# Key masks and counts read from PSUM, the first pass's maximum transposed in float32 and added by a one-row product, and another order of preparation and weights

## The chip, the cores and the metric

The kernel runs on one core of a Trainium2 chip. The metric is the device time of one execution in microseconds (us), as the median of several runs. The engines are TensorE (PE in the profile; its weight loads are PEld), VectorE (DVE), ScalarE (ACT), GpSimd (POOL) and SyncE (SP), which issues all DMAs here.

## The reference

Attention over 4 batches x 8 heads x 768 tokens x 64 dimensions, in which a query sees only the keys of its own cluster, and then a feed-forward block over the 3072 tokens:

```python
q_assign = np.argmax(np.einsum('bhsd,hcd->bhsc', q_n, c_n), axis=-1)      # 16 clusters per head
k_assign = np.argmax(np.einsum('bhsd,hcd->bhsc', k_n, c_n), axis=-1)
mask = q_assign[:, :, :, None] == k_assign[:, :, None, :]
scores = scale * np.matmul(q, k.transpose(0, 1, 3, 2))
scores = np.where(mask, scores, -1000000000.0)
attn = softmax(scores)                                                    # row maximum subtracted
x = matmul(attn, v), heads side by side: (3072, 512)
h = x @ w_in                                                              # (3072, 2048)
g = np.maximum(h, 0.0) + np.log1p(np.exp(-np.abs(h)))
out = g @ w_out                                                           # (3072, 512)
```

A row whose cluster holds no key has all its scores masked alike, so it must average all values.

## The kernel before

**Precision.** Operands of large products are split into two float16 numbers (a high and a low part), and a product is made of three matmuls. The weights come as 64-bit floats, and are rebuilt into such halves by shifts on VectorE, copies on ScalarE and a subtraction on GpSimd (32 weight steps, `prep_weights`, tiles `wi` and `wo`).

**Tiles.** A pass is half of a batch's queries: 8 passes, each with 8 heads x 3 tiles of 128 queries, 192 tiles in all. In the 7 passes from the second on (168 tiles), `scores` makes a tile of 128 queries x 768 keys (`s`), VectorE takes the negated maximum (`negm`), ScalarE the exponential (`p`) and its float16 half (`phl`), GpSimd the rest; a transposing DMA turns two tiles at once (`pt<-phl`), and `attend` multiplies them with the values (`vb`) into PSUM (`mbank`). The first pass (24 tiles) goes through `upright`: a product `m` over the 96 rows of the second half of the operands gives a maximum that is good enough, which is transposed on TensorE (`mT`), copied under the queries' rows (`qt`), and subtracted inside the score product `u`, whose rows are keys; so no DMA has to turn them, and `ptf` is multiplied with the raw float32 values (`rawv`). The feed-forward block (`ffn1`: `h<-xT,wi`; softplus; `ffn2`: `o<-wo,gh`) of a pass runs beside the attention of later passes.

**Masks.** `prep_k` and `prep_q` find the nearest centroid of each key and query (`nearest`, tile `sim` in PSUM, 16 columns per tile). They write mask columns beside the 64 columns of the operand (`n2`: 64 to 79), which are transposed with it: 0 or -65504 on the key's side (`MASK`), 65504 on the query's side. The same score product then masks. `clusters` counts the keys of each cluster by a product with a tile of ones; the flag `al` says which clusters have any, and `prep_q` multiplies the query's own column with it.

**Order.** Each engine runs its instructions in the order in which they were emitted. That order is made at build time by the class `Order`: each chain of operations has a priority (the tile `t` at which it is due, with offsets), each operation an assumed duration, and the operation that can start first is emitted, the lower priority first at a tie. Where the plan leaves TensorE idle for over 600 ns, `warm` emits dummy products (`mbank<-ones,eye`, 128x120) for 0.65 of the gap, at 52 ns each. An operation marked `shared` waits in the plan for a marked operation of the other one of VectorE and GpSimd. Rings of buffers (`od.get`, `ring`) set how far a chain can run ahead: `mc` has 2 buffers, `h` and `s` in PSUM 2 each, `o` 1. A transposing DMA (`flip`) is planned at 180 ns a block, with 900 ns ahead and 1500 ns behind; `pt` has 24 blocks.

Of the kernel before, what the change touches and what calls it, by code (L numbers as in the profile page):

```python
# [8 lines left out]
F16 = mybir.dt.float16  # L9
# [11 lines left out]
LAG = 4  # L21
AHEAD = 10
# [6 lines left out]
SHIFT_BY = (2048.0, 1.0)  # L29
KROWS = SHIFT + 2  # L30
# [88 lines left out]
def tile_cluster_attention__then__softplus_ffn(  # L119
# [59 lines left out]

    ones = cpool.tile([P, P], F16, name="ones")  # L180
# [9 lines left out]
    for i in range(2):  # L190
        t = cpool.tile([P, 2 * NT, P], F16, name=f"n2_{i}")
        nc.gpsimd.memset(t[:, :, D + NCL :], 0.0)
        for c, m in zip(range(SHIFT, KROWS), SHIFT_BY):
            nc.gpsimd.memset(t[:, :, c : c + 1], m)
        N2.append(t)

    MC = []
    for i in range(2):
        t = cpool.tile([P, KROWS], F16, name=f"mc_{i}")
        nc.gpsimd.memset(t, 0.0)  # L200
        MC.append(t)


    od = Order()

# [27 lines left out]
    def flip(dst, src, blocks):  # L233

        return op(
            "SP", 150 * blocks + 100, lambda: nc.sync.dma_start_transpose(out=dst, in_=src), dma=180.0 * blocks
        )
# [59 lines left out]
    def prep_weights(step: int):  # L297
# [32 lines left out]
        yield op("ACT", 630, lambda: nc.scalar.activation(mag, val, AF.Prelu, scale=sc, alpha=SIGN_UP))  # L330
# [8 lines left out]
        yield op("ACT", 610, lambda: nc.scalar.copy(part[:, 0], val))  # L339
# [22 lines left out]
    def prep_v(n: int):  # L362
# [14 lines left out]
        if n < H:  # L377
            od.cur["prio"] = H * QT
# [36 lines left out]
    def nearest(xs, heads, low: int, sfx: str, twin: int):  # L415
# [26 lines left out]
        yield op("DVE", 345, lambda: nc.vector.tensor_reduce(mx, sim, AX.X, ALU.max))  # L442
        yield op("DVE", 345, lambda: nc.vector.tensor_tensor(sim, sim, mx.to_broadcast(shp), ALU.is_equal))
        yield op("DVE", 345, lambda: nc.vector.tensor_tensor(sim, sim, tab.to_broadcast(shp), ALU.mult))
        best = p2.tile([P, nt, 1], F32, tag="best", name=f"best_{sfx}")
        yield op("DVE", 345, lambda: nc.vector.tensor_reduce(best, sim, AX.X, ALU.max))
# [8 lines left out]
    def prep_k(n: int):  # L455

        kkey[n // 2] = yield from ring("kt", NP)
        if n in (4, 6):
# [25 lines left out]
        eq = p2.tile([P, 2 * NT, NCL], F16, tag="eq", name=f"eq_k{n}")  # L484
        yield op("DVE", 345, lambda: nc.vector.tensor_tensor(eq, sim, best, ALU.is_equal))
        yield op(
            "DVE",
            450,
            lambda: nc.vector.tensor_scalar(n2[:, :, D : D + NCL], eq, 1.0, MASK, ALU.subtract, ALU.mult),
            shared=True,  # L490
        )
        od.spawn(clusters(n, ps, eq, hk), od.cur["prio"])
        yield from turn(kt[:, 1].rearrange("p h c t -> p (h c) t"), n2, f"kT1_{n}", n < NPE)
        od.set(n2k)
        od.set(("k", n))

    def clusters(n, ps, eq, hk):
# [3 lines left out]
        yield op("PE", 100, lambda: nc.tensor.matmul(cnt, ones, eq, start=True, stop=True))  # L501
        if n - h % 4 not in alive:
            alive[n - h % 4] = p2.tile([P, 4, NCL], F16, tag="al", name=f"al_{n}", bufs=4)
        al = alive[n - h % 4][:, h % 4 : h % 4 + 2]
        yield op(
            "DVE", 345, lambda: nc.vector.tensor_reduce(al, cnt.rearrange("p (u c) l -> p u l c", u=2), AX.X, ALU.max)
        )
        od.set(hk)
        yield op("DVE", 300, lambda: nc.vector.tensor_scalar(al, al, 1.0, None, ALU.min), shared=True)
        od.set(("al", n))  # L510

    def prep_q(n: int, pi: int):
# [10 lines left out]
        for u in range(4):  # L523
# [19 lines left out]
        yield op("DVE", 345, lambda: nc.vector.tensor_tensor(sim, sim, best, ALU.is_equal))  # L543
# [4 lines left out]
            345,  # L548
            lambda: nc.vector.tensor_tensor(
                sim4, sim4, al.unsqueeze(2).to_broadcast([P, 4, QT, NCL]), ALU.mult  # L550
            ),
        )
        yield op("DVE", 345, lambda: nc.vector.tensor_scalar(n2[:, :, D : D + NCL], sim, MASK, None, ALU.mult))
# [3 lines left out]
        yield op("DVE", 345, lambda: nc.vector.tensor_reduce(aq, sim, AX.X, ALU.max))  # L557
# [17 lines left out]
    def upright(t: int):  # L575
# [19 lines left out]
        mk = yield from ring("mc", 2)  # L595
        mc = MC[mk[2] % 2]
        negm = p2.tile([P, 1], F32, tag="negm", name=f"negm_{sfx}", bufs=4)
        yield op("DVE", 950, lambda: nc.vector.tensor_reduce(negm, st[:, :, :SH], AX.XY, ALU.max, negate=True))
        od.set(sk)
        top, rest = mc[:, SHIFT : SHIFT + 1], mc[:, SHIFT + 1 : SHIFT + 2]  # L600
        by = SHIFT_BY[0]
# [3 lines left out]
        ps = ps_h.tile([P, P], F16, tag="h", name=f"mT_{sfx}")  # L605
        yield op("PE", 60, lambda: nc.tensor.transpose(out=ps[:KROWS], in_=mc, identity=eye))
        od.set(mk)
        yield op("ACT", 250, lambda: nc.scalar.copy(qt[SHIFT:KROWS, 1, i], ps[SHIFT:KROWS]))
# [6 lines left out]
        def emit():  # L615
            for c in range(NT):
                to = up[:, c // (NT // 2), c % (NT // 2) * P : (c % (NT // 2) + 1) * P]
                nc.tensor.matmul(to, kt[:, 0, c], qt[:, 0, i], start=True, stop=False)
                nc.tensor.matmul(to, kt[:KROWS, 1, c], qt[:KROWS, 1, i], start=False, stop=True)

        yield op("PE", 690, emit)
        od.set(("sc", t))
        if i == QT - 1 and n % 2 and passes[pi][1] + QT == NT:
# [87 lines left out]
    def attend(t: int):  # L711
# [29 lines left out]
        if h % 2 == 0 or i < QT - 1:  # L741
            return
        if pi == 0:
# [68 lines left out]
    def softplus(pi, f, hp, hk):  # L812
# [4 lines left out]
        yield op("ACT", 500, lambda: nc.scalar.activation(a, hp, AF.Exp))  # L817
# [145 lines left out]
```

## Time and profile before

| | us |
|---|---|
| median of 3 runs | 867.36 (865.41 to 870.8) |
| the profiled execution, its own time | 867.29 |
| its span, from the first to the last instruction | 865.5 |
| TensorE busy in the span | 838.4 (97%) |
| VectorE, ScalarE, GpSimd busy | 480.7, 575.3, 524.0 |

A busy time is the union of the instructions' spans. A product's span is much longer than the distance to the next one, since products are pipelined: what a stream of products costs is read from the starts in the timeline. Windows are stretches of the span, with the busy time and the number of instructions of each engine; a number behind x is a count.

### The profile page before, as it was taken

What the parts mean: (1) busy time and instruction counts of PE and PEld (TensorE: products, weight loads), DVE (VectorE), ACT (ScalarE), POOL (GpSimd) and SP (SyncE); (2) the same over time, 40 slices, a digit from 0 to 9 for tenths busy, and PEclk for the clock granted to TensorE, in tenths of its full rate; (3) what the DMA queues carried; (4) which work ended last, traced back from release to release, by engine and by line L of the source; (5) the groups of instructions that cost most, each with busy time, mean ns of one, the idle gap of its engine ahead of it and who ended that gap; (6) DMA issues with size and microseconds to landing.
All of it is one profiled execution on the core that took longest, in us unless ns stands there. A gap on an engine that the chain in (4) does not pass through costs nothing.

```text
span 865.5 us, 20493 instructions
## 1 busy us (share of the span) xinstructions
PE 838.4 (97%) x8539; PEld 546.1 (63%) x8539; DVE 480.7 (56%) x924; ACT 575.3 (66%) x880; POOL 524.0 (61%) x362
## 2 busy tenths in 40 slices
PE   7799899999999999999999999999999999999997
PEld 7689886566566666555656666666666656655554
DVE  6887866666657545655655646667554534321211
ACT  5677587885778876857757878667776667533330
POOL 5523447887677787764847797668676666512120
PEclk9999999999999999999999999999999999999999
DMA  9623759999899999998969999999898767610000
GB/s 254 239 84 102 168 122 197 232 219 229 163 203 182 196 182 204 219 196 159 158 133 165 190 195 193 204 224 168 175 156 174 125 120 143 123 20 14 24 1 36
DMA packets 398509, 136.11 MB, mean 157 GB/s; under 512 B 375888, under 2 KB 391248, under 8 KB 398416
## 3 DMA queue, kind: packets, MB, share of 16 engines
q1 hardware_dynamic: 398416, 134.80, 78.9%
q8 instruction: 66, 1.08, 0.5%
q14 instruction: 27, 0.22, 0.1%
HBM read 35.68 MB, written 6.29 MB: 48 GB/s over the span
## 4 chain that ended last, share of the span: by engine, by line
PE 67%; issue 10%; POOL 4%; ACT 2%; DVE 2%; DMA 1%; POOLq 0%; ACTq 0%; DVEq 0%
PE s L661 11%; PE o L865 7%; PE o L867 7%; PE o L866 7%; PE h L801 7%; PE h L803 7%; PE h L802 7%; PE mbank L733 3%; PE mbank L735 3%; PE mbank L734 3%; POOL gh L839 2%; POOL phl L691 1%; DMA pt<-phl 1%; ACT p L680 1%; DVE negm L677 1%
## 5 line engine op out<-in xcount | busy, mean ns | idle before, releaser
L691 POOL TENSOR_TENSOR phl<-p,phl 128x768 f16<-128x768 f32 x168 | 276.1, 1657 | 101.2 <-ACT phl L689 79.3
L677 DVE TENSOR_REDUCE negm<-s 128x1 f32<-128x768 f32 x168 | 160.2, 956 | 98.6 <-PE s L661 96.5
L680 ACT ACTIVATE p<-s,negm 128x768 f32<-128x768 f32 x168 | 150.7, 899 | 55.4 <-DVE negm L677 37.9
L839 POOL TENSOR_TENSOR gh<-fg,gh 128x768 f16<-128x768 f32 x64 | 105.9, 1654 | 121.3 <-ACT gh L838 120.7
L803 PE MATMUL h<-xT,wi 128*128 128x384 f16 x512 | 166.7, 326 | 0.0
L801 PE MATMUL h<-xT,wi 128*128 128x384 f16 x512 | 166.6, 325 | 0.0
L802 PE MATMUL h<-xT,wi 128*128 128x384 f16 x512 | 166.6, 325 | 0.0
L817 ACT ACTIVATE fa<-h 128x384 f32<-128x384 f32 x128 | 62.4, 490 | 127.3 <-PE h L803 126.8
L867 PE MATMUL o<-wo,gh 128*128 128x512 f16 x384 | 145.5, 379 | 1.0 <-POOL gh L839 1.0
L865 PE MATMUL o<-wo,gh 128*128 128x512 f16 x384 | 145.4, 379 | 0.5 <-DVE ot L881 0.2
L866 PE MATMUL o<-wo,gh 128*128 128x512 f16 x384 | 145.4, 379 | 0.0
L827 DVE SCALAR_TENSOR_TENSOR fg<-fa,h 128x384 f32<-128x384 f32 x128 | 70.4, 550 | 133.1 <-ACT fa L818 132.6
L689 ACT CAST phl<-p 128x768 f16<-128x768 f32 x168 | 135.0, 829 | 14.0 <-DMA pt<-phl 13.2
L661 PE MATMUL s<-kt,qt 128*128 128x384 f16 (+1 forms) x672 | 136.0, 325 | 2.8 <-ACT p L680 2.3
L733 PE MATMUL mbank<-vb,pt 128*128 128x65 f16 x1008 | 108.7, 192 | 1.5 <-DMA pt<-phl 1.5
L734 PE MATMUL mbank<-vb,pt 128*128 128x64 f16 x1008 | 108.6, 192 | 0.0
L735 PE MATMUL mbank<-vb,pt 128*128 128x65 f16 x1008 | 108.4, 194 | 0.0
L733 PEld LDWEIGHTS <-pt 128*128 128x128 f16 x1008 | 93.5, 98 | 15.2 <-DMA pt<-phl 3.3
L734 PEld LDWEIGHTS <-pt 128*128 128x128 f16 x1008 | 92.9, 97 | 11.3
L735 PEld LDWEIGHTS <-pt 128*128 128x128 f16 x1008 | 92.9, 97 | 0.0
L661 PEld LDWEIGHTS <-qt 128*128 128x128 f16 (+1 forms) x672 | 62.7, 98 | 45.0 <-issue 3.4
L803 PEld LDWEIGHTS <-wi 128*128 128x128 f16 x512 | 49.8, 97 | 33.4
(128 smaller groups left out, 1260.4 us busy)
## 6 DMA issues: line engine op xcount, KB each, us to landing
wo<-in_moe_w_in_dram SPq DMA_DIRECT2D x16, 512.0 KB, 6.4
wo<-in_moe_w_out_dram SPq DMA_DIRECT2D x14, 512.0 KB, 4.0
rawk<-in_k_dram SPq DMA_DIRECT2D x16, 384.0 KB, 4.6
rawq<-in_q_dram SPq DMA_DIRECT2D x16, 384.0 KB, 4.3
out_dram<-ot SPq DMA_DIRECT2D x24, 256.0 KB, 2.5
rawv<-in_v_dram SPq DMA_DIRECT2D x12, 384.0 KB, 3.9
rawv<-in_v_dram SPq DMA_DIRECT2D x8, 192.0 KB, 6.0
pt<-phl SPq DMA_TRANSPOSE x84, 6.2
```

The lines of the kernel that those rows point to most:

```text
L661: nc.tensor.matmul(st[:, j, :SH], qt[:rows, s, i], kt[:rows, s, NT // 2 * j : NT // 2 * (j + 1)], start=(s == 0), stop=(s == 1),)
L677: yield op("DVE", 950, lambda: nc.vector.tensor_reduce(negm, st[:, :, :SH], AX.XY, ALU.max, negate=True))
L691: "POOL", 1640, lambda: nc.gpsimd.tensor_tensor(phl[:, u, 1], p32, phl[:, u, 0], ALU.subtract), shared=True
L733: nc.tensor.matmul(av, pt[:, 0, c], vb[:, c, D : 2 * D + 1], start=(c == 0), stop=False)
L734: nc.tensor.matmul(av[:, :D], pt[:, 0, c], vb[:, c, :D], start=False, stop=False)
L735: nc.tensor.matmul(av, pt[:, 1, c], vb[:, c, D : 2 * D + 1], start=False, stop=(c == NT - 1))
L801: nc.tensor.matmul(hp, w[0], x[0], start=(c == 0), stop=False)
L802: nc.tensor.matmul(hp, w[0], x[1], start=False, stop=False)
L803: nc.tensor.matmul(hp, w[1], x[0], start=False, stop=(c == NP - 1))
L865: nc.tensor.matmul(po, g[0], wo[:, f, 0, 0], start=(f == f0), stop=False)
L866: nc.tensor.matmul(po, g[0], wo[:, f, 0, 1], start=False, stop=False)
L867: nc.tensor.matmul(po, g[1], wo[:, f, 0, 0], start=False, stop=(f == f0 + NF // 2 - 1))
```

## The change

**Masks of the keys.** The comparison with the best centroid is written over `sim` in PSUM (float32) and no longer into a float16 tile `eq`; the mask columns are made from it, no longer from `eq`, and the operation is no longer marked `shared`. The count is made of two products into one sum, the mask columns and a constant column of 65504 (`every`), so it comes as a multiple of 65504; `al` is kept in float32, its `min` with 1 is gone, and `prep_q` takes the `min` of its 0 or 1 with it instead of a product, after the query's mask columns have been written rather than before.

**The maximum of the first pass.** The two VectorE operations that split it into two float16 columns of `mc` are gone. The float32 maximum (now `negu`, a ring of 4) is broadcast to 97 columns and transposed in float32, with a float32 identity `eye32` that lies in a buffer of the tag `ot` until the last tile of the first pass. ScalarE copies one row, times 1/65504, and each 128-key piece of `u` has three products: 96 rows, 128 rows, and one row (row 96, against the 65504 of the keys).

**Order.** Assumed durations change by a few per cent, and the numbers at the top set when chains are due.

```diff
-LAG = 4
-AHEAD = 10
+LAG = 5
+AHEAD = 6
+K_FROM = 15
+Q_FROM = 10
+V_FROM = 6
+V_SPLIT = 36
+W_AT = 16
+W_STEP = 0.6
+SECOND = 6
+POST = 2
...
-SHIFT_BY = (2048.0, 1.0)
-KROWS = SHIFT + 2
+KROWS = SHIFT + 1
...
+    eye32 = p2.tile([P, P], F32, tag="ot", name="eye32", bufs=QT)
+    nc.gpsimd.tensor_copy(eye32, eye)
...
-            "SP", 150 * blocks + 100, lambda: nc.sync.dma_start_transpose(out=dst, in_=src), dma=180.0 * blocks
+            "SP", 150 * blocks + 100, lambda: nc.sync.dma_start_transpose(out=dst, in_=src), dma=155.0 * blocks
...
-        eq = p2.tile([P, 2 * NT, NCL], F16, tag="eq", name=f"eq_k{n}")
-        yield op("DVE", 345, lambda: nc.vector.tensor_tensor(eq, sim, best, ALU.is_equal))
...
-            lambda: nc.vector.tensor_scalar(n2[:, :, D : D + NCL], eq, 1.0, MASK, ALU.subtract, ALU.mult),
-            shared=True,
-        )
-        od.spawn(clusters(n, ps, eq, hk), od.cur["prio"])
+        yield op("DVE", 355, lambda: nc.vector.tensor_tensor(sim, sim, best, ALU.is_equal))
+        other = n2[:, :, D : D + NCL]
+        yield op("DVE", 355, lambda: nc.vector.tensor_scalar(other, sim, 1.0, MASK, ALU.subtract, ALU.mult))
+        every = n2[:, :, SHIFT:KROWS].to_broadcast([P, 2 * NT, NCL])
+        od.spawn(clusters(n, ps, other, every, hk), od.cur["prio"])
...
-        yield op("PE", 100, lambda: nc.tensor.matmul(cnt, ones, eq, start=True, stop=True))
+            nc.tensor.matmul(cnt, ones, other, start=True, stop=False)
+            nc.tensor.matmul(cnt, ones, every, start=False, stop=True)
...
-        yield op("DVE", 300, lambda: nc.vector.tensor_scalar(al, al, 1.0, None, ALU.min), shared=True)
...
-        mk = yield from ring("mc", 2)
+        mk = yield from ring("negu", 4)
...
-        yield op("DVE", 90, lambda: nc.vector.tensor_scalar(top, negm, 1.0 / by, None, ALU.mult))
-        yield op("DVE", 90, lambda: nc.vector.scalar_tensor_tensor(rest, top, -by, negm, ALU.mult, ALU.add))
...
-        yield op("PE", 60, lambda: nc.tensor.transpose(out=ps[:KROWS], in_=mc, identity=eye))
+            lambda: nc.tensor.transpose(out=ps[:KROWS], in_=negm.to_broadcast([P, KROWS]), identity=eye32),
...
-                nc.tensor.matmul(to, kt[:, 0, c], qt[:, 0, i], start=True, stop=False)
-                nc.tensor.matmul(to, kt[:KROWS, 1, c], qt[:KROWS, 1, i], start=False, stop=True)
+                nc.tensor.matmul(to, kt[:SHIFT, 1, c], qt[:SHIFT, 1, i], start=True, stop=False)
+                nc.tensor.matmul(to, kt[:, 0, c], qt[:, 0, i], start=False, stop=False)
+                nc.tensor.matmul(to, kt[SHIFT:KROWS, 1, c], qt[SHIFT:KROWS, 1, i], start=False, stop=True)
...
+        od.cur["prio"] = t + POST
...
-                od.spawn(prep_k(n), w - 12)
+                od.spawn(prep_k(n), w - K_FROM)
...
-                od.spawn(prep_q(n, pi), w - 11.5)
+                od.spawn(prep_q(n, pi), w - Q_FROM)
...
-        od.spawn(prep_weights(step), begin - 12 + step * 0.6)
+        od.spawn(prep_weights(step), W_AT + step * W_STEP)
...
-            (begin + pi * per + per / 2 * (half + 1) + 3 + per / 2 / QT * i, ffn2(pi, half, i))
+            (begin + pi * per + per / 2 * (half + 1) + SECOND + per / 2 / QT * i, ffn2(pi, half, i))
```

What the change does to the engines' streams is shown at three places. In all of them a name with a number is one buffer: `sim_k_308` is the scores against the centroids of the keys of heads 0 and 1, `sim_k_360` (after: `sim_k_300`, `sim_k_353`) those of heads 2 and 3.

The first place is VectorE at the start, from the masks of the first four heads' keys to the first copies of the transposed queries. Before:

```order
L485 TENSOR_TENSOR eq_k_426<-sim_k_360,best_k_423 128x192
L489 TENSOR_SCALAR n_0_110<-eq_k_416 128x12x16
L489 TENSOR_SCALAR n_1_114<-eq_k_426 128x12x16
L506 TENSOR_REDUCE al_500<-sim_k_308 128x32
L506 TENSOR_REDUCE al_500<-sim_k_360 128x32
L509 TENSOR_SCALAR al_500<-al_500 128x32 x2
L332 TENSOR_SCALAR wi<-wi 128x512 x2
L336 SCALAR_TENSOR_TENSOR wo<-wo,wi 128x512
L408 COPY qt_0_306<-qT_0_0_6_525 128x768
```

And in the change:

```order
L490 TENSOR_SCALAR n_0_112<-sim_k_300 128x12x16
L450 TENSOR_REDUCE best_k_416<-sim_k_353 128x12
L488 TENSOR_TENSOR sim_k_353<-sim_k_353,best_k_416 128x192
L513 TENSOR_REDUCE al_459<-sim_k_300 128x32
L490 TENSOR_SCALAR n_1_115<-sim_k_353 128x12x16
L513 TENSOR_REDUCE al_459<-sim_k_353 128x32
L336 TENSOR_SCALAR wi<-wi 128x512
L412 COPY qt_0_298<-qT_0_0_6_510 128x768
```

The two `min` operations on `al` are gone, the masks read `sim`, and one weight shift stands ahead of the queries' copy where two shifts and a merge stood.

The second place is GpSimd at the start: the rest of the weights (`wi`), the values' low halves (`vb`) and the product of the queries with their flag (`n<-qn,aq`), for which the first score product waits. Before:

```order
L383 TENSOR_TENSOR vb_106<-rawv_134,vb_106 128x12x64
L383 TENSOR_TENSOR vb_108<-rawv_135,vb_108 128x12x64
L340 TENSOR_TENSOR wi<-wo,wi 128x512 x3
L562 TENSOR_TENSOR n_0_110<-qn_0_0_307,aq_0_617 128x12x64
L470 TENSOR_TENSOR kn_4_622<-rawk_615,kn_4_622 128x12x64
```

And in the change:

```order
L387 TENSOR_TENSOR vb_108<-rawv_130,vb_108 128x12x64
L387 TENSOR_TENSOR vb_110<-rawv_131,vb_110 128x12x64
L344 TENSOR_TENSOR wi<-wo,wi 128x512 x2
L569 TENSOR_TENSOR n_0_112<-qn_0_0_299,aq_0_594 128x12x64
L344 TENSOR_TENSOR wi<-wo,wi 128x512
L474 TENSOR_TENSOR kn_4_598<-rawk_592,kn_4_598 128x12x64
```

The third weight step has moved behind the queries' product.

The third place is TensorE in the first pass, the start of the second tile's `u`. Before:

```order
L618 LDWEIGHTS kt_138
L618 MATMUL u_1_917<-qt_0_306,kt_138 128x128
L619 LDWEIGHTS kt_138
L619 MATMUL u_1_917<-qt_0_306,kt_138 128x128
L618 LDWEIGHTS kt_138
```

And in the change:

```order
L628 LDWEIGHTS kt_134
L628 MATMUL u_1_849<-qt_0_298,kt_134 128x128
L629 LDWEIGHTS kt_134
L629 MATMUL u_1_849<-qt_0_298,kt_134 128x128
L630 LDWEIGHTS kt_134
L630 MATMUL u_1_849<-qt_0_298,kt_134 128x128
L628 LDWEIGHTS kt_134
```

The product of line 630 is new; it has one row and sits at row 96 of the array. Over the whole stream TensorE has 836 dummy products before and 645 in the change. Until the first `m` product there are 322 before and 307 in the change, from there to the last `u` 186 and 86, from there to the last pass's end 272 and 212, and 56 and 40 in the gap near the very end. On VectorE 901 rows become 843, and SP's first two loads are both of keys where a load of values stood between them.

More of the change, by code (lines that the diff above doesn't have):

```diff
@@ L192, in tile_cluster_attention__then__softplus_ffn @@
         nc.gpsimd.memset(t[:, :, D + NCL :], 0.0)
-        for c, m in zip(range(SHIFT, KROWS), SHIFT_BY):
-            nc.gpsimd.memset(t[:, :, c : c + 1], m)
+        nc.gpsimd.memset(t[:, :, SHIFT:KROWS], MASK)
         N2.append(t)
[L197 to L201, printed above, removed]
     od = Order()
+    eye32_key = od.get("ot", QT)[1]
     mbank = ps_m.tile([P, 512], F32, name="mbank")
@@ L329, in prep_weights @@
             yield wait("wr", rooms[f // 2])
-        yield op("ACT", 630, lambda: nc.scalar.activation(mag, val, AF.Prelu, scale=sc, alpha=SIGN_UP))
+        yield op("ACT", 670, lambda: nc.scalar.activation(mag, val, AF.Prelu, scale=sc, alpha=SIGN_UP))
         od.set(("wd", step))
@@ L338, in prep_weights @@
         )
-        yield op("ACT", 610, lambda: nc.scalar.copy(part[:, 0], val))
+        yield op("ACT", 655, lambda: nc.scalar.copy(part[:, 0], val))
         yield op("POOL", 1160, lambda: nc.gpsimd.tensor_tensor(part[:, 1], val, part[:, 0], ALU.subtract), shared=True)
@@ L377, in prep_v @@
         if n < H:
[L378 removed]
+            od.cur["prio"] = V_SPLIT
         yield op("ACT", 830, lambda: nc.scalar.copy(vb[:, :, :, D : 2 * D], vf))
@@ L542, in prep_q @@
         ps, sim, best = yield from nearest([qt0[:, c] for c in range(c12)], heads, 1, f"q{sfx}", TWIN * (pi > 0))
-        yield op("DVE", 345, lambda: nc.vector.tensor_tensor(sim, sim, best, ALU.is_equal))
+        yield op("DVE", 358, lambda: nc.vector.tensor_tensor(sim, sim, best, ALU.is_equal))
+        yield op("DVE", 358, lambda: nc.vector.tensor_scalar(n2[:, :, D : D + NCL], sim, MASK, None, ALU.mult))
         sim4 = sim.rearrange("p (u c) l -> p u c l", u=4)
@@ L547, in prep_q @@
             "DVE",
-            345,
+            360,
             lambda: nc.vector.tensor_tensor(
-                sim4, sim4, al.unsqueeze(2).to_broadcast([P, 4, QT, NCL]), ALU.mult
+                sim4, sim4, al.unsqueeze(2).to_broadcast([P, 4, QT, NCL]), ALU.min
             ),
         )
-        yield op("DVE", 345, lambda: nc.vector.tensor_scalar(n2[:, :, D : D + NCL], sim, MASK, None, ALU.mult))
         if pi == 0:
@@ L556, in prep_q @@
         aq = p2.tile([P, c12, 1], F16, tag="aq", name=f"aq_{sfx}")
-        yield op("DVE", 345, lambda: nc.vector.tensor_reduce(aq, sim, AX.X, ALU.max))
+        yield op("DVE", 358, lambda: nc.vector.tensor_reduce(aq, sim, AX.X, ALU.max))
         od.set(hk)
```

50 lines of the change are left out of this document (29 added, 21 removed).

## The prediction, made before the changed kernel was run

> **What bounds the kernel now.** I read the busy times, then windows by stage, then the same windows for the dummy products alone.
>
> ```profile
> PE 838.4 (97%) x8539; PEld 546.1 (63%) x8539; DVE 480.7 (56%) x924; ACT 575.3 (66%) x880; POOL 524.0 (61%) x362
> 0.00:37.00 37.00, 28.18 (x474) 26.71 (x475) 28.21 (x81) 20.55 (x31) 18.96 (x30) 0.95 0.88 279
> 37.00:125.00 88.00, 81.56 (x1012) 74.13 (x1010) 69.22 (x163) 63.36 (x107) 36.67 (x30) 0.98 0.42 109
> 125.00:275.00 150.00, 143.16 (x1628) 94.09 (x1628) 97.76 (x175) 113.25 (x170) 110.73 (x75) 1.00 1.06 205
> 275.00:825.00 550.00, 549.82 (x5213) 332.28 (x5210) 278.69 (x495) 369.94 (x561) 352.74 (x227) 1.00 0.83 154
> 825.00:866.00 41.00, 35.72 (x222) 18.90 (x220) 6.79 (x11) 8.16 (x15) 4.91 (x3) 1.00 0.05 20
> ```
>
> The columns of a window are its length and the busy time of PE, PEld, DVE, ACT and POOL, then the granted clock. From 275 to 825 us TensorE is never idle, so there only fewer products would help, and the change takes none away. All that can be won lies in the first 275 us and in the last 40: the start (8.8 us idle), the first pass (6.4), the filling of the feed-forward pipeline (6.8), the end (4.8 of a span that ends at 865.5, 4 of them behind the last product). The dummies are idle time too, painted over:
>
> ```profile
> 0.00:37.00 37.00, 20.38 (x322) 19.18 (x322) 0.95 0.88 279
> 37.00:125.00 88.00, 12.87 (x199) 11.60 (x199) 0.98 0.42 109
> 125.00:275.00 150.00, 16.04 (x259) 14.73 (x259) 1.00 1.06 205
> 14.17 3.68 PE L214 MATMUL mbank<-ones,eye 128*128 128x120 f16 x67
> ```
>
> A dummy costs (3.68 - 0.22) / 66 = 52.4 ns of stream (0.22 is the span of the last one). The program holds them whether they are needed or not.
>
> **The start, to the first `m` product.** A chain of dependent operations sets when it begins, at 36.55 us:
>
> ```profile
> 36.55 0.81 PE L585 MATMUL m<-kt,qt 96*128 96x384 f16 x4
> PE qT L404 <- POOL n L562: 2.9, 1, 2.9
> PE qT L404 <- ACT wi L330: 2.3, 1, 2.3
> L489 DVE TENSOR_SCALAR n<-eq_k x16: 197/422/1633, 17.9 to 599.5; 128x192 f16<-128x192 f16 x16
> 17.93 2.39 DVE L489 TENSOR_SCALAR n<-eq_k 128x192 f16<-128x192 f16 x2
> 20.78 2.63 DVE L509 TENSOR_SCALAR al<-al 128x32 f16<-128x32 f16 x2
> 24.59 0.55 DVE L408 COPY qt<-qT 128x768 f16<-128x768 f16 x1
> 26.62 0.36 DVE L442 TENSOR_REDUCE mx_q<-sim_q 128x12 f32<-128x192 f32 x1
> 17.11 6.27 POOL L383 TENSOR_TENSOR vb<-rawv,vb 128x768 f16<-128x768 f32 x4
> ```
>
> Two masks took 2.39 us and two `min` over 32 columns 2.63, while GpSimd was in `vb`; the same mask operation takes 0.20 at its shortest, so these were blocked, not working. The change reads PSUM instead, as the reduction of 0.36 us above does: two masks cost 0.72, the two `min` nothing, and VectorE is free 4.3 us earlier. Not all of that arrives. The queries' copies also hang on ScalarE, which waited for a weight load:
>
> ```profile
> 19.93 0.66 ACT L330 ACTIVATE wi<-wo 128x512 f32<-128x512 f32 x1 [1.82 <-DMA wo<-in_moe_w_in_dram]
> 21.22 0.67 ACT L330 ACTIVATE wi<-wo 128x512 f32<-128x512 f32 x1
> 21.80 0.77 ACT L410 COPY qt<-qT 128x768 f16<-128x768 f16 x1
> 31.32 1.69 POOL L340 TENSOR_TENSOR wi<-wo,wi 128x512 f16<-128x512 f32 x1 [1.33 <-ACT wi L339]
> 32.97 1.65 POOL L562 TENSOR_TENSOR n<-qn,aq 128x768 f16<-128x768 f16 x1
> 2.37 0.63 SPq L231 DMA_DIRECT2D rawk<-in_k_dram  x1
> ```
>
> That load still stands ahead. Of the two weight activations behind it one moves away, so the copy of `qt` starts some 0.6 us earlier, and the three VectorE copies (0.56 each) then follow TensorE, not the weight operations: I put `sim_q` 1.4 us earlier (bounds 0.6, ScalarE's share, and 4.3, all of VectorE's). On GpSimd the weight step that ran from 31.32 to 32.97 moves behind the product `n`: another 1.6. The keys' load moves one place ahead on SP, worth at most one issue, 0.6; I take 0.3. Together **-3.3**, with the 15 fewer dummies and the four doubled counts already inside, for this stretch is as long as its chain. Bounds: -6.6 and -1.0.
>
> **The first pass.** New on TensorE are a third product in each of 24 x 6 pieces, and a float32 transpose for a float16 one.
>
> ```profile
> 43.34 0.22 PE L618 MATMUL u<-qt,kt 128*128 128x128 f16 x1
> 43.98 0.22 PE L619 MATMUL u<-qt,kt 98*128 98x128 f16 x1
> 66.18 1.45 PE L729 MATMUL mbank<-rawv,ptf 128*128 128x65 f32 x12
> L729 PE MATMUL mbank<-rawv,ptf 128*128 128x65 f32 x288 | 36.1, 276 | 0.3 <-ACT ptf L637 0.2
> ```
>
> The first and the last of 12 products of `u` start 0.64 us apart: 58 ns each, whether 128 or 98 rows. 144 x 58 = **+8.35**. No row has a product of one row. Below, it could run beside its neighbour (0, at worst); above, it could make TensorE empty itself before and after. A product lasts 0.22 us from start to end, so that costs (220 - 58) ns at each of 288 changes, +46.7. I take 58, the nearest row, since 98 and 128 rows alternate there without a loss.
>
> A float32 product of 65 columns is two records (288 for 24 x 6) of 106 ns each ((1.45 - 0.28) / 11). For 128 columns one record would be 209, two 418; the transpose of before costs 57. I take one: 24 x 152 = **+3.7** (0 to +8.7). The Trainium skill, "TensorE: Matmul & The Clock Gate", section "Terms", says that a transpose mode makes float32 four times faster. By it 418 becomes 105, and the term would be +1.2 rather than +3.7; no run here shows a float32 transpose.
>
> Gone on VectorE, which is busy for 69 of these 88 us, are
>
> ```profile
> 37.00:125.00 88.00, 7.35 (x24) 0.98 0.42 109
> 37.00:125.00 88.00, 3.38 (x24) 0.98 0.42 109
> 37.00:125.00 88.00, 0.35 (x2) 0.98 0.42 109
> 37.00:125.00 88.00, 1.34 (x2) 0.98 0.42 109
> L606 PE MATMUL mT<-eye,mc x24: 216/219/311, 41.5 to 117.9; 128*98 128x128 f16 x24
> ```
>
> the two split operations (lines 603 and 602, 10.7 us), the 0.35 of two `min`, and 1.34 - 0.72 of two masks: 11.7 us, and for each tile 0.45 us between its maximum and its transpose. The ring of 4 instead of 2 also lets maxima run ahead of their transposes. What it brings is on TensorE: the program holds 100 dummies fewer here, 100 x 52.4 = **-5.2**, and the idle time between them goes with them, 6.44 us beside 199 dummies or 32 ns each: **-3.2** (bounds 0, and -6.4, all of it). The stage comes to 8.35 + 3.7 + 0.2 (two more counts of 80 ns) - 5.2 - 3.2 = +3.8.
>
> **From there to 825 us.** Twelve counts have a second product of 192 columns; half of a 384-column one, by the four `m` products above, is (0.81 - 0.33) / 3 / 2 = 80 ns: **+1.0**. 60 dummies fewer: **-3.1**. Idle time beside them, 6.84 us for 259 or 26 ns each: **-1.6** (0 to -3). The `min` of later batches,
>
> ```profile
> 125.00:866.00 741.00, 7.59 (x12) 1.00 0.83 157
> ```
>
> saves nothing, because TensorE is full there; without that cover it would be worth its 7.6 us at most.
>
> The new numbers cost something here. A flip of `pt` is now planned at 24 x 155 + 2400 = 6.1 us, before at 6.7, and it takes
>
> ```profile
> L236 SPq DMA_TRANSPOSE pt<-phl x84: 3500/3990/5418, 125.3 to 753.4; - x84
>   DMA pt<-phl: 4.8, 7
> DMA to landing us min/median/max: 5.4/6.2/8.0
> ```
>
> 6.2 at the median. So half of the 84 flips land after the plan's time, by up to 1.9 us, and the value products stand in TensorE's order as if they had not; behind one that waits stands all of TensorE. Before, that cost 4.8 us of idle time in 7 places (over both of its sequences). `LAG` 5 for 4 puts other products between. I take **+1.0** (0 to +13).
>
> **The end.** 16 dummies fewer, -0.8, and 0.8 us of idle time by 16/56, -0.2: **-1.0**.
>
> **The sum** is made against the profiled execution's 867.3, which is within 0.1 us of the median, with the 1.8 us around its span left as they are: -3.3 + 3.8 + 1.0 - 3.1 - 1.6 + 1.0 - 1.0 = -3.2, so **864 us**. A per cent, 8.7 us, is about what a measurement of this kernel tells from no change.
>
> **Rivals.**
>
> *The pass empties TensorE (0.15).* The one-row products sit in one 32-row strip; if each change between strip and whole array lets the stream run dry, the first pass gains 46.7 us of TensorE time, and dummies, being instructions, don't give way; only its idle time, 3.2 after the change, does. 864 + 46.7 - 3.2 = 907. It decides from about 40 ns a change (+11.5), and half the price gives 884. Against it: nothing in the trace; 98 rows after 128 lose nothing, but they aren't confined to a strip. The Trainium skill, "TensorEngine Tiling (Array Packing)", section "Key Properties", states that changing the tiling mode drains TensorE; no run of before shows a change of mode, so it can neither agree nor differ.
>
> *More comes of VectorE (0.17).* The first pass is bound by its chain from maximum to `u`, all 6.4 us of its idle time go, and the third product fits beside its neighbour: 864 - 8.35 - 3.2 = 852. For it: 69 busy us of 88 on VectorE. Against it: TensorE itself was busy for 81.6, 10.4 of them dummies.
>
> *The waits stay (0.12).* Fewer dummies are only fewer dummies, and the idle time of 3.2 + 1.6 + 0.2 us and the start's 3.3 come back elsewhere: 864 + 8.3 = 872.
>
> *The value products meet their weights late (0.09).* With 0.3 us at each of the 42 late flips, 12.6 instead of 1.0: 876, the point from which it is slower.
>
> **How the numbers follow.** The forecast has 0.47, with a range of its own from 857 to 871: the bounds of the start (-3.3 and +2.3), of the transpose (-3.7 and +5.0) and of the pass's idle time (-3.2 and +3.2), not all at once. For 8 in 10 the range reaches over the second rival below to 851, and above over the fourth and half of the price of the first, to 884; outside are the full price of the first and the best part of the second. Faster by over 1% (below 858.7): the second rival and 0.08 of the forecast, 0.25. Slower by over 1% (above 876): the first rival and half of the fourth, 0.2. Within 1%: 0.55.
>
> **What would show it.** The first `m` product starts near 33 us, and the two masks there take 0.7 us. In the timeline 18 products of `u` take 1.04 us; 3 us would be the first rival, 0.7 the second. The float32 transpose stands 210 ns ahead of the next product (100 by the skill, 420 for two records). TensorE's idle time in the first pass falls to about 3 us, and from 275 us on stays under 1 us; if it shows several us behind `pt<-phl`, the flip's number was too short. The forecast is wrong if the one-row products cost anything but 58 ns, or if the waits of the first pass only change their names.

## The result, and the profile after

The changed kernel takes **959.55 us** at the median of 4 runs (950.75 to 965.04), the kernel before 867.87 beside it: a ratio of 1.1021 (95% interval 1.092 to 1.1122). Its profiled execution took 955.69 us, the span in it is 953.9. The forecast was 864, its range ended at 884. Slow executions (965.04 here, two of the four with half the changes, and single ones of 1233.11 us of the kernel before and 4721.77 us of the best one) are in the medians of this document and left out of its ratios.

The page of the changed kernel, its busy times and its row of the granted clock (40 slices of 23.8 us):

```profile
PE 926.2 (97%) x8508; PEld 589.2 (62%) x8508; DVE 456.2 (48%) x860; ACT 579.2 (61%) x880; POOL 522.8 (55%) x359
PEclk9955575569999999999999999999999999999999
```

And the row of the clock in the kernel before:

```profile
PEclk9999999999999999999999999999999999999999
```

TensorE runs 31 instructions fewer than before and is busy for 88 us more. Before, every slice of the clock stood at 9. Now seven slices in a row, from 48 to 214 us, stand at 5 to 7: that is the first pass, which lasts from 33 to 203 us. The windows of the changed kernel, by stage (length, busy PE, PEld, DVE, ACT, POOL, granted clock, DMA share, GB/s):

```profile
0.00:46.00 46.00, 37.48 (x567) 32.02 (x567) 35.25 (x91) 28.59 (x44) 24.44 (x30) 1.00 0.77 241
46.00:128.00 82.00, 81.52 (x502) 59.80 (x500) 29.12 (x60) 28.33 (x48) 15.01 (x13) 0.50 0.12 38
138.00:158.00 20.00, 20.00 (x100) 14.94 (x98) 7.90 (x15) 4.92 (x11) 2.58 (x2) 0.50 0.19 39
163.00:206.00 43.00, 43.00 (x223) 29.41 (x221) 10.12 (x17) 16.64 (x25) 13.22 (x10) 0.50 0.31 66
375.00:910.00 535.00, 533.52 (x5038) 320.90 (x5036) 258.49 (x471) 360.80 (x538) 336.29 (x218) 1.00 0.81 153
```

For 82 us TensorE works at half its clock, then for 20, then for 43, and in all of it the profile shows it busy with hardly a pause: 81.52 of 82, 20 of 20, 43 of 43 us. From 375 us on the clock is that of before, and TensorE's share nearly so.

Where the 88.4 us of span went is read from three marks, the first product `m`, the last product `u`, and the end. These are the rows of the two tiles in the changed kernel (times of the first and the last start behind the three durations):

```profile
L592 PE MATMUL m<-kt,qt x48: 323/524/528, 32.6 to 161.3; 96*128 96x384 f16 x48
L630 PE MATMUL u<-qt,kt x144: 224/282/285, 37.9 to 203.2; 1*128 1x128 f16 x144
```

And in the kernel before:

```profile
L619 PE MATMUL u<-qt,kt x144: 216/219/311, 43.4 to 122.5; 98*128 98x128 f16 x144
```

The start is 4.0 us shorter (32.6 for 36.6). The first pass, from the first `m` to the last `u`, takes 170.6 us for 85.9: +84.7. From the last `u` to the end it is 750.7 for 743.0: +7.7. The three make 88.4.

What fills the first pass is seen in its products one by one. The timeline of the changed kernel, at full clock and at half (start, length, line, tile):

```profile
37.69 0.22 PE L628 MATMUL u<-qt,kt 96*128 96x128 f16 x1
37.75 0.22 PE L629 MATMUL u<-qt,kt 128*128 128x128 f16 x1
37.90 0.22 PE L630 MATMUL u<-qt,kt 1*128 1x128 f16 x1
38.05 0.23 PE L628 MATMUL u<-qt,kt 96*128 96x128 f16 x1
...
90.44 0.29 PE L628 MATMUL u<-qt,kt 96*128 96x128 f16 x1
90.52 0.31 PE L629 MATMUL u<-qt,kt 128*128 128x128 f16 x1
90.76 0.28 PE L630 MATMUL u<-qt,kt 1*128 1x128 f16 x1
90.98 0.29 PE L628 MATMUL u<-qt,kt 96*128 96x128 f16 x1
...
164.96 2.82 PE L742 MATMUL mbank<-rawv,ptf 128*128 128x65 f32 x12
```

At full clock the product of 128 rows follows that of 96 rows after 0.06 us, as all did before. The one-row product follows after 0.15, and the next product of 96 rows after another 0.15: some 97 ns are lost on each change into the strip and each change out of it. A piece takes 0.36 to 0.38 us instead of 0.116. At half clock the piece takes 0.54 (0.08, 0.24, 0.22). And the half clock strikes the neighbours too: a tile's six float32 value products, 12 records, last 2.82 us, before 1.45. By starts, waits left out, `u` takes 71 us of the stream for 17 before, and the float32 value products 58 for 32: +54 and +26 of the 84.7.

### The profile page after: what moved, and what is told of

Same layout as the page of the kernel before. It is cut to its first block, busy times and chain, and to the rows that moved or that the text cites. A ratio compares the mean times of both kernels' runs of the same rounds, so it can differ in the third digit from the quotient of the medians.

```text
span 953.9 us, 20389 instructions
## 1 busy us (share of the span) xinstructions
PE 926.2 (97%) x8508; PEld 589.2 (62%) x8508; DVE 456.2 (48%) x860; ACT 579.2 (61%) x880; POOL 522.8 (55%) x359
## 4 chain that ended last, share of the span: by engine, by line
PE 78%; DMA 9%; issue 4%; DVE 4%; POOL 2%; ACT 2%; POOLq 0%; SPq 0%; DVEq 0%; ACTq 0%
PE s L674 10%; PE o L879 7%; PE o L880 7%; PE o L881 7%; PE h L815 7%; PE h L817 7%; PE h L816 7%; DMA pt<-phl 7%; PE mbank L742 6%; PE u L630 3%; PE u L628 3%; PE mbank L746 3%; PE mbank L748 3%; PE mbank L747 3%; PE mbank L218 2%
## 5 line engine op out<-in xcount | busy, mean ns | idle before, releaser
L702 ACT CAST phl<-p 128x768 f16<-128x768 f32 x168 | 138.0, 831 | 13.9 <-DMA pt<-phl 11.9
L674 PE MATMUL s<-kt,qt 128*128 128x384 f16 (+1 forms) x672 | 141.0, 333 | 2.0 <-ACT p L693 1.9
```

Source lines behind the costliest of these rows:

```text
L674: nc.tensor.matmul(st[:, j, :SH], qt[:rows, s, i], kt[:rows, s, NT // 2 * j : NT // 2 * (j + 1)], start=(s == 0), stop=(s == 1),)
```

## The experiments

The theory (S): a one-row product at row 96 sits in a strip of the array, the 32 rows from row 96 on, and each change between strip and whole array lets the stream run dry; with 288 such changes in a pass TensorE's granted clock falls to half, and everything else in the pass pays for that. The rivals: the third product as such costs it, wherever it sits; the other order, or the float32 transpose, starves the pass, and the clock falls because of that; what matters for the gate is how few rows work, not the changes. For the remaining 7.7 us the rivals were the planned number of the flips against the other numbers of the order.

**Without the strip.** Two products of the whole array, 128 rows and 97, all else as in the change:

```diff
-                nc.tensor.matmul(to, kt[:SHIFT, 1, c], qt[:SHIFT, 1, i], start=True, stop=False)
-                nc.tensor.matmul(to, kt[:, 0, c], qt[:, 0, i], start=False, stop=False)
-                nc.tensor.matmul(to, kt[SHIFT:KROWS, 1, c], qt[SHIFT:KROWS, 1, i], start=False, stop=True)
+                nc.tensor.matmul(to, kt[:, 0, c], qt[:, 0, i], start=True, stop=False)
+                nc.tensor.matmul(to, kt[:KROWS, 1, c], qt[:KROWS, 1, i], start=False, stop=True)
```

> The changed kernel with the one-row product folded back into the 96-row one: two products per piece of u (128 rows, and 97 rows), so no product sits in a strip of the array. The order of all else stays. Theory S (the strip: each change between strip and whole array costs about 100 ns, and the gaps let the clock fall to half for most of the first pass): the clock stays at 1.0 outside short dips, and the time falls from 959 to about 856, the 864 of the forecast less 8.35 for the third product. Rival O (the new order with 191 fewer dummies lets the clock fall): the clock falls as in the changed kernel, the time stays above 920. Rival F (the float32 transposes let it fall): above 920 as well.

Measured: 867.09 us, ratio 0.9989 (0.9972 to 1.0006). The windows of this kernel, and its rows on `u` and `pt`:

```profile
33.00:115.00 82.00, 75.42 (x900) 68.03 (x898) 66.19 (x115) 63.76 (x109) 37.01 (x30) 1.00 0.43 122
115.00:275.00 160.00, 145.11 (x1639) 95.19 (x1636) 100.33 (x177) 118.19 (x181) 118.31 (x79) 0.99 1.03 197
...
L629 PE MATMUL u<-qt,kt x144: 219/219/222, 37.7 to 114.8; 97*128 97x128 f16 x144
...
  DMA pt<-phl: 17.2, 21
```

The clock is back at 1.00, with the new order, the float32 transpose and the scaled copy still there: without the strip none of these makes it fall. The last `u` starts at 114.8, 7.7 us earlier than before. But the time is that of before, some 11 us above what had been expected: the gain is lost again behind the last `u`, where TensorE waits 17.2 us for `pt` in 21 places (before 4.8 in 7).

**Three products, none in a strip.** The first of them is overwritten by the second and is extra work alone:

```diff
-                nc.tensor.matmul(to, kt[:SHIFT, 1, c], qt[:SHIFT, 1, i], start=True, stop=False)
-                nc.tensor.matmul(to, kt[:, 0, c], qt[:, 0, i], start=False, stop=False)
-                nc.tensor.matmul(to, kt[SHIFT:KROWS, 1, c], qt[SHIFT:KROWS, 1, i], start=False, stop=True)
+                nc.tensor.matmul(to, kt[:SHIFT, 1, c], qt[:SHIFT, 1, i], start=True, stop=True)
+                nc.tensor.matmul(to, kt[:, 0, c], qt[:, 0, i], start=True, stop=False)
+                nc.tensor.matmul(to, kt[:KROWS, 1, c], qt[:KROWS, 1, i], start=False, stop=True)
```

> The changed kernel with three products per piece of u, all on the whole array: 96 rows (its result is overwritten), 128 rows, 97 rows. The number of products and the order are those of the changed kernel. Theory S: 58 ns a product, no fall of the clock in the first pass, 864 us, 8 us above the kernel with two products. Rival N (a third product is too much for the first pass, strip or not): above 920.

Measured: 873.37 us, ratio 1.0053 (1.0028 to 1.0078). Its timeline:

```profile
37.56 0.22 PE L628 MATMUL u<-qt,kt 96*128 96x128 f16 x1
37.62 0.22 PE L629 MATMUL u<-qt,kt 128*128 128x128 f16 x1
37.68 0.22 PE L630 MATMUL u<-qt,kt 97*128 97x128 f16 x1
37.74 0.22 PE L628 MATMUL u<-qt,kt 96*128 96x128 f16 x1
```

0.06 us apart, all of them: 6.3 us more than with two products, where the prediction's term for a third was 8.35. The number of products is not what costs the 92 us.

**The strip alone, on the kernel before.** Its second product is split into 96 rows and a strip of its two last rows, nothing else is changed:

```diff
-                nc.tensor.matmul(to, kt[:, 0, c], qt[:, 0, i], start=True, stop=False)
-                nc.tensor.matmul(to, kt[:KROWS, 1, c], qt[:KROWS, 1, i], start=False, stop=True)
+                nc.tensor.matmul(to, kt[:SHIFT, 1, c], qt[:SHIFT, 1, i], start=True, stop=False)
+                nc.tensor.matmul(to, kt[:, 0, c], qt[:, 0, i], start=False, stop=False)
+                nc.tensor.matmul(to, kt[SHIFT:KROWS, 1, c], qt[SHIFT:KROWS, 1, i], start=False, stop=True)
```

> The kernel before, with its 98-row product split into 96 rows and a two-row product at row 96, nothing else: three products a piece, the last in a strip. Theory S: the strip alone does the damage: 18 products of u take about 2.2 us at the full clock instead of 0.70, the clock falls to half for most of the first pass, 940 to 970 us. Rivals O and F: this kernel has neither the new order nor a float32 transpose, so about 876 (867 and 8.35 for the third product).

Measured: 955.89 us, ratio 1.1019 (1.0971 to 1.1068), the ratio of the whole change. Its windows:

```profile
76.00:151.00 75.00, 75.00 (x456) 55.43 (x456) 26.59 (x66) 22.68 (x39) 13.30 (x12) 0.50 0.21 59
158.00:212.00 54.00, 54.00 (x283) 36.53 (x282) 14.65 (x28) 17.86 (x29) 9.91 (x8) 0.50 0.20 55
```

The same half clock at a busy TensorE, without the float32 transpose and in the old order. The strip alone is enough.

**A strip of 32 rows instead of one:**

```diff
-                nc.tensor.matmul(to, kt[SHIFT:KROWS, 1, c], qt[SHIFT:KROWS, 1, i], start=False, stop=True)
+                nc.tensor.matmul(to, kt[SHIFT:, 1, c], qt[SHIFT:, 1, i], start=False, stop=True)
```

> The changed kernel with the strip's product made of all its 32 rows (row 96 and 31 rows of zeros) instead of one. Theory S: a change costs the same whatever the strip holds, 945 to 970 us with the clock at half for most of the first pass. Rival 1 (a product of one row is the slow thing): about 864.

Measured: 958.82 us, ratio 1.1045 (1.1002 to 1.1087). Its timeline:

```profile
37.43 0.22 PE L628 MATMUL u<-qt,kt 96*128 96x128 f16 x1
37.49 0.22 PE L629 MATMUL u<-qt,kt 128*128 128x128 f16 x1
37.64 0.22 PE L630 MATMUL u<-qt,kt 32*128 32x128 f16 x1
37.80 0.23 PE L628 MATMUL u<-qt,kt 96*128 96x128 f16 x1
```

The same spacings to 0.01 us: how many rows of the strip work makes no difference. A product of few rows that starts at row 0 was not tried.

**Half the changes.** The pieces go in twos, four products of the whole array and then two one-row products side by side: 144 changes a pass, with as many one-row products as in the change.

```diff
-            for c in range(NT):
...
+            for group in ((0, 3), (1, 4), (2, 5)):
...
+                for c in group:
+                    nc.tensor.matmul(to[c], kt[:SHIFT, 1, c], qt[:SHIFT, 1, i], start=True, stop=False)
+                    nc.tensor.matmul(to[c], kt[:, 0, c], qt[:, 0, i], start=False, stop=False)
+                for c in group:
+                    nc.tensor.matmul(to[c], kt[SHIFT:KROWS, 1, c], qt[SHIFT:KROWS, 1, i], start=False, stop=True)
```

> The changed kernel with the pieces of u taken in twos (one in each bank of PSUM): four products on the whole array, then two one-row products, so 6 changes a tile instead of 12, 144 in all, with the same 144 one-row products. Theory S with the gaps seen in the changed kernel (about 97 ns a change at the full clock): 14 us of gaps instead of 28; whether the clock falls is the question. If the gaps hold it down, it falls for part of the first pass, 890 to 930 us; if the one-row products themselves do (rival K), it falls as before, 950 and more.

Measured: 909.37 us (895.5 to 921.6), ratio 1.035 (1.0302 to 1.0398). Its windows:

```profile
46.00:115.00 69.00, 66.59 (x739) 53.13 (x738) 44.57 (x87) 40.56 (x72) 21.20 (x18) 1.00 0.35 96
115.00:160.00 45.00, 43.49 (x249) 32.52 (x249) 13.88 (x22) 22.32 (x32) 16.99 (x13) 0.51 0.34 83
```

Now most of the pass keeps the full clock, and 45 us of it fall. At full clock two pieces take 0.54 us instead of 0.23, or 22 us for the pass: 867 + 22 = 889. The profiled execution took 901.6, which leaves some 13 for the fallen clock. The wide spread of the four times goes with the clock: they are 895.5, 901.6, 917.2 and 921.6 us at mean clocks of 0.982, 0.972, 0.959 and 0.946. With a clock of either 1 or a half, that is some 32, 50, 75 and 99 us at half clock, so by this estimate each of them lengthens the run by some 0.4 us.

**48 changes.** Two one-row products of 384 columns at the head of each tile, then the twelve others:

```diff
+            for j in range(2):
+                bank = up[:, j, :SH].rearrange("p (c t) -> p c t", c=NT // 2)
+                nc.tensor.matmul(bank, kt[SHIFT:KROWS, 1, 0], top, start=True, stop=False)
```

> The changed kernel with the one-row products of a tile put into two of 384 columns, ahead of the twelve others: 2 changes a tile between strip and whole array instead of 12, 48 in all. Theory S: the price goes with the changes, 48 x 0.1 = 5 us more than the same work on the whole array, and the gaps are too few to hold the clock down: 856 to 872 us. Rival K (a product of one row itself counts as idle for the clock, however it is ordered): the strips still stream 768 columns a tile, the clock falls in the first pass, above 920.

Measured: 877.45 us, ratio 1.0107 (1.0068 to 1.0145), the clock 0.997 over the run. Its timeline:

```profile
40.87 0.49 PE L629 MATMUL u<-qt,kt 1*128 1x384 f16 x2
41.30 0.23 PE L632 MATMUL u<-qt,kt 96*128 96x128 f16 x1
41.36 0.22 PE L633 MATMUL u<-qt,kt 128*128 128x128 f16 x1
...
41.95 0.22 PE L633 MATMUL u<-qt,kt 128*128 128x128 f16 x1
```

A tile takes 41.95 + 0.06 - 40.87 = 1.14 us; twelve products at 0.058 are 0.70. The difference for 24 tiles is 10.6. The last `u` starts at 123.3 for 114.8 with two products, 8.5 us later, and the granted clock was 1.00 up to there: this price is stream and not clock. Most of it is the strips' own columns: a product of 384 columns takes 0.16 us to the next one, so two of them in 24 tiles take some 8 us. The run is 10.4 us above the one with two products, and 5 above the 872 that had been expected at most.

**Why the kernel without the strip gains nothing.** First its length in the plan, which the first of these runs had left at 1050 ns:

```diff
-        yield op("PE", 1050, emit)
+        yield op("PE", 690, emit)
```

> The changed kernel with two products per piece of u on the whole array, and the plan told so (690 ns instead of 1050). Of the change it leaves out the one-row product alone. The kernel with two products in the changed kernel's order gave 867 us: 10 us earlier at the first ffn1 product than before (128 for 138 us), and all of it lost from there to 275 us. Theory D (the flip's number: value products stand too early in TensorE's order and wait for their transposed weights, 17 us in 21 places): the same here, 862 to 868. Rival W (the plan was only spoilt by the wrong 1050): the waits go, 855.

Measured: 866.99 us, ratio 0.9992 (0.9976 to 1.0008), and 17.9 us behind `pt` in 18 places. That was not it. The first pass did change: with 690 the plan puts 224 dummies there for 86, and the last `u` starts at 122.9, 8.0 us later than with 1050, at the same time for the whole. Then, on this kernel, the flips planned at 180 ns a block again:

```diff
-            "SP", 150 * blocks + 100, lambda: nc.sync.dma_start_transpose(out=dst, in_=src), dma=155.0 * blocks
+            "SP", 150 * blocks + 100, lambda: nc.sync.dma_start_transpose(out=dst, in_=src), dma=180.0 * blocks
```

> The run with two products planned, with one number put back: a flip's 180 ns a block instead of 155. The other new numbers stay. Theory D: value products move 1 to 2 us away from their scores in TensorE's order, the idle time behind pt falls from 17 us to under 8, the time to 856 to 861. Rival A (the shorter distance between attention and feed-forward, AHEAD 6 and SECOND 6, leaves too little to fill the waits with): pt waits fall but the time stays at 864 to 868.

Measured: 862.18 us, ratio 0.9927 (0.99 to 0.9953): 4.8 us less, just short of the 856 to 861 expected. Its rows on `u` and `pt`:

```profile
L629 PE MATMUL u<-qt,kt x144: 216/219/222, 37.9 to 123.8; 97*128 97x128 f16 x144
...
  DMA pt<-phl: 2.2, 4
```

The waits for `pt` fall by 15.7 us, the time by a third of that.

And all of the old order, the flips and the other numbers:

```diff
-LAG = 5
-AHEAD = 6
-K_FROM = 15
+LAG = 4
+AHEAD = 10
+K_FROM = 12
...
-V_SPLIT = 36
-W_AT = 16
+V_SPLIT = 24
+W_AT = 22
...
-            "SP", 150 * blocks + 100, lambda: nc.sync.dma_start_transpose(out=dst, in_=src), dma=155.0 * blocks
+            "SP", 150 * blocks + 100, lambda: nc.sync.dma_start_transpose(out=dst, in_=src), dma=180.0 * blocks
```

> The kernel of the run with two products planned, with the order numbers of before (LAG 4, AHEAD 10, the old due times, 180 ns a block): masks and counts from PSUM and the float32 transpose alone. Theory D: the start and the first pass keep their gain, and waits behind pt fall back to about 5 us: 857 to 861. Rival P (the preparation's gain is lost wherever TensorE meets attention's own pace, whatever the order): 866 to 868.

Measured: 867.11 us, ratio 0.9988 (0.9974 to 1.0001), where 857 to 861 had been expected, and 866 to 868 by the rival that the gain is lost wherever TensorE meets attention's own pace. The waits for `pt` are gone here too (3.2 us in 7 places), but the last `u` starts only at 127.2:

```profile
L629 PE MATMUL u<-qt,kt x144: 216/219/222, 38.5 to 127.2; 97*128 97x128 f16 x144
```

The gain of the start is there (`u` begins at 38.5 for 43.4), and the old order, with 284 dummies in the first pass for 186 before, gives it back there. Whether that is what holds the time at 867 is not shown. The order numbers alone, on the kernel before, the short flips with them:

```diff
-LAG = 4
-AHEAD = 10
+LAG = 5
+AHEAD = 6
+K_FROM = 15
...
-            "SP", 150 * blocks + 100, lambda: nc.sync.dma_start_transpose(out=dst, in_=src), dma=180.0 * blocks
+            "SP", 150 * blocks + 100, lambda: nc.sync.dma_start_transpose(out=dst, in_=src), dma=155.0 * blocks
```

> The kernel before with the new order numbers alone (LAG, AHEAD, due times, POST, SECOND, 155 ns a block). Theory D: the first pass has none of its gain and the waits behind pt rise: 870 to 878. Rival G (the new numbers are the part that gains, by starting weights and feed-forward sooner): 858 to 864.

Measured: 869.77 us, ratio 1.0015 (0.9996 to 1.0034), not clear of no change. Its row on `pt`:

```profile
  DMA pt<-phl: 23.1, 27
```

The last `u` starts 5.9 us earlier than before (116.6), and 18.3 us more of waiting for `pt` stand against that. Over all kernels of this study, the waits for `pt` are 9.7 to 23.1 us in the eight that plan a flip at 155 ns a block, and 1.1 to 5.2 in the six that plan it at 180.

**The best of these parts:** two products, the new order, the plan's length of 1050 for `u`, and the flips at 180.

```diff
-            "SP", 150 * blocks + 100, lambda: nc.sync.dma_start_transpose(out=dst, in_=src), dma=155.0 * blocks
+            "SP", 150 * blocks + 100, lambda: nc.sync.dma_start_transpose(out=dst, in_=src), dma=180.0 * blocks
```

> Two products per piece of u on the whole array, all new order numbers but the flip's (180 ns a block again), and the changed kernel's 1050 ns left in the plan for u. The run with 690 ns gave 862. With 1050 ns the plan puts fewer dummies into the first pass (some 4.5 us instead of 11), and that pass was 8 us shorter with the flips at 155. Theory D and this: 855 to 859. Rival (what the first pass gains, the filling of the feed-forward pipeline gives back, since attention's own pace sets it): 861 to 863.

Measured: **860.76 us**, ratio 0.9911 (0.9885 to 0.9937), 0.9% faster than the kernel before. Its windows, `u` and `pt`:

```profile
115.00:275.00 160.00, 152.66 (x1738) 101.79 (x1736) 100.06 (x179) 118.27 (x178) 114.53 (x77) 1.00 1.01 193
...
L629 PE MATMUL u<-qt,kt x144: 218/219/222, 37.9 to 115.2; 97*128 97x128 f16 x144
...
  DMA pt<-phl: 1.6, 4
```

The first pass ends as early as with the short flips, and TensorE stands still for 7.3 us between 115 and 275 instead of 14.9. But 855 to 859 had been expected, and 861 to 863 by the rival that what the first pass gains is given back behind it. The time lies at this rival's edge: beside the run with flips at 180 and a planned 690 ns, the last `u` starts 8.6 us earlier (115.2 for 123.8), and the whole is 1.4 us shorter. What sets the pace from there to 275 us was not tried apart.

**Fewer dummies.** The same kernel with dummies for 0.3 of a planned gap, 335 instead of 750:

```diff
-WARM_SHARE = 0.65
+WARM_SHARE = 0.3
```

> The same with WARM_SHARE 0.3 instead of 0.65: 335 dummies instead of 750, in the same order. If dummies cost stream time, as the prediction had it (52 ns each): up to 22 us less, at most what stands in gaps that end sooner than planned, 848 to 856. If they only fill waits: the same time. If the clock needs them: it falls in the start or the first pass, 865 to 890.

Measured: 864.05 us, ratio 0.9946 (0.9924 to 0.9969), 3.3 us slower than with all of them. Its row of the clock and the window of its start:

```profile
PEclk9799999999999999999999999999999999999999
0.00:46.00 46.00, 32.17 (x382) 28.21 (x383) 33.96 (x91) 28.97 (x45) 24.72 (x30) 0.85 0.77 236
```

415 dummies at 52 ns would be 22 us of stream. None of that comes back: in the first 33 us, worked out from the starts of all products, the dummies fall from some 16 us to 7, and the waits grow from some 9 to 18. And the clock falls in the start, to 0.85 over 46 us.

## Why the prediction was wrong, point by point

**The start (-3.3) was right in its steps, less so in their sizes.** It is 4.0 shorter, and the rows of the changed kernel show the steps:

```profile
17.48 0.34 DVE L490 TENSOR_SCALAR n<-sim_k 128x192 f16<-128x192 f32 x1
18.66 0.35 DVE L490 TENSOR_SCALAR n<-sim_k 128x192 f16<-128x192 f32 x1
28.54 1.92 POOL L569 TENSOR_TENSOR n<-qn,aq 128x768 f16<-128x768 f16 x1
32.56 0.81 PE L592 MATMUL m<-kt,qt 96*128 96x384 f16 x4
```

The two masks take 0.69 us (0.72 forecast, 2.39 before), the queries' product starts 4.4 us earlier, `m` at 32.56 for "near 33". `sim_q` came 2.6 us earlier (24.06 for 26.62), where the forecast had 1.4: ScalarE's weight operation, which it took to stand ahead as before, came at 17.63 for 19.93. The order numbers had little part in it: with them alone `m` starts at 36.4, with the new masks and counts in the old order at 33.3.

**The third product (+8.35) is the step that failed.** Its price, "I take 58, the nearest row, since 98 and 128 rows alternate there without a loss", is right for a third product of the whole array (6.3 us) and wrong for one in a strip. The forecast named the rival for it, "The pass empties TensorE", with a chance of 0.15, and said itself that the alternating rows "aren't confined to a strip". That is the sentence that should have moved the chance: the row chosen as nearest was no neighbour in what mattered. The rival's mechanism is the one that holds. Its price per change was too high, 162 ns for 97: at full clock the pieces cost 144 x (0.376 - 0.116) = 37 us more, where it had 55 with the third product's own time. A tile's 18 products took 2.2 us at full clock, between the 1.04 of the forecast and the rival's 3. Without the clock that would have been about 867 + 37 = 904, an estimate; that the rival's 907 is so close is luck, since its strips were some 14 us too dear and the kernel without them some 11 us too cheap. What it lacked altogether is the clock: the rest, up to the 955.7 of the profiled execution, comes with the half clock, which also stretches the float32 value products by 26 us. The Trainium skill, "TensorEngine Tiling (Array Packing)", section "Key Properties", says that changing the tiling mode drains TensorE. Here the trace agrees, at 97 ns a change.

**The transpose (+3.7) was about +2.** In the kernel of two products at full clock the next product mostly starts 0.14 us behind it:

```profile
36.28 0.30 PE L611 MATMUL mT<-eye,negu 128*97 128x128 f32 x1
36.42 0.33 PE L592 MATMUL m<-kt,qt 96*128 96x384 f16 x1
```

The forecast had 0.21; 24 x (0.14 - 0.057) = 2.0 us. The estimate from the section "Terms" of the Trainium skill's page "TensorE: Matmul & The Clock Gate" was 0.105, and the measurement lies between the two.

**The dummies (-5.2 in the pass) shortened the pass, and not the time.** The first pass without the strip came out near the forecast, 82.3 us for 85.9 (-3.7, where the sum without the third product had 3.8 - 8.35 = -4.6). The price of a dummy was right there: 138 more of them, with the plan's length of `u` alone changed, made the pass 8.0 us longer, 58 ns each. The idle time beside them (-3.2) did not go: it was 82.00 - 75.42 = 6.6 us for 6.4 before. But those two kernels took 867.09 and 866.99 us. The forecast took what TensorE saves in the pass off the time of the whole kernel, and that step failed too, hidden under the larger ones. The last run shows the other side: where a dummy fills a wait, taking it away leaves the wait, and its loss can cost the clock.

**The value products (+1.0) were the second failed step.** The row that gave it was right, landings of 6.2 us at the median for a plan of 6.1, and so was the mechanism; the size was not. In the changed kernel:

```profile
  DMA pt<-phl: 16.4, 23
...
DMA to landing us min/median/max: 5.4/6.0/8.4
```

16.4 us for 4.8: +11.6, within the bound of +13 and near the fourth rival's 12.6; 38 of the 84 flips landed after more than the planned 6.1 us. "`LAG` 5 for 4 puts other products between" was hope: 180 ns a block, tried alone, takes 15.7 us of these waits away and 4.8 us off the time. From the last `u` on the forecast summed to -3.7, and +7.7 came; without the waits for `pt` that would be -4.7 and -3.9.

Together: -0.7 in the start, +80.9 in the first pass and +11.4 behind it are the 91.6 us between the forecast's -3.2 and the +88.4 of the profiled span.

## What to carry to other kernels

A product on few rows is not a small product: first ask whether it runs in the same mode as its neighbours, as 96, 97, 98 and 128 rows from row 0 did here, or sits in a strip, as 1, 2 or 32 rows from row 96 on did. If it must sit there, group it: 2 strip products a tile, next to each other, cost 10 us here, most of it their own columns, and 6 apart cost 88. Where a plan stands an instruction at the moment a transfer is expected to land, plan with the slow landings and not with the median, since one late landing stops the whole engine behind it. Dummies that fill waits are not time to be won. And a stage that ends earlier need not shorten the kernel: 8 to 9 us less in the first pass were worth 0 to 1.4 us at the end.

## What the runs showed of the hardware that was not expected

The granted clock fell to half while the profile showed TensorE busy for 81.52 of 82 us. In the windows that lie within one such stretch it was 0.50, never between. 288 changes in the pass brought it about in three kernels, 144 for 45 us, 48 not at all; after `u` ended, it came back. The Trainium skill, "TensorE: Matmul & The Clock Gate", section "Part 1: The HAM clock gate (the "warmup" mystery)", has a gate of 4/8 or 8/8 that follows how busy TensorE has been, and falls after an idle window of some 3.4 us. The two values agree, and so does the length: in all fourteen traces the clock's changes lie whole steps of 3.41 us apart, and the three stretches of the changed kernel are 24, 6 and 13 steps long. Single steps at half clock stand in every kernel but the best one, the kernel before included (101 to 104 us). The idle window is not in this trace, since the clock stayed down with TensorE shown busy for 99% of the time.

What decides a step's clock can be counted from the starts of all products: it goes by the columns that TensorE streamed in the step before. Take a column of a float32 value product as four (two in each of its two records) and one in the strip as nothing. Then fewer than 3,150 columns, of some 7,900 in a full step, mean half clock in the next step and more mean full clock, in 3,403 of the 3,412 steps of the fourteen traces up to 840 us, and at 59 of the 64 changes of the clock (a step's columns counted from 0.1 us before it). With the strip's columns counted in full the misses are 18 for 9. This is a rule fitted to these traces, its two weights included, and no kernel was made to test it. By it the clock fell because the array streamed too little between the changes, and stayed down because at half clock it streams still less: 2,240 columns a step from 46 to 128 us in the changed kernel, for 5,190 in the one with two products.

The price of a change is that of the mode and not of the work: 0.15 us from start to start going in and 0.15 coming out, beside 0.06 without a change, for a strip with 1 row and with 32 alike.
